# Attention over packed queries with a feed-forward block: another order of the first batch's steps, two more fillers' worth of matmuls at the start, some pieces on another engine

## The chip, the cores and the metric

The kernel runs on one core of one Trainium2 chip. The metric is the device time of one execution in microseconds. The core has the engines TensorE (PE; its weight loads are shown apart, as PEld), VectorE (DVE), ScalarE (ACT) and GpSimd (POOL), and SyncE (SP), which issues the transfers. Each works through its own list of instructions in order and waits on semaphores for the others.

## The reference

For 8 batches of 8 heads, 576 tokens and a head size of 64, 32 packed queries per head attend to all tokens, and then the tokens attend to the 32 packed results:

```python
def sm_attn(qq, kk, vv):
    s = scale * np.matmul(qq, kk.transpose(0, 1, 3, 2))
    s = s - np.max(s, axis=-1, keepdims=True)
    a = np.exp(s)
    a = a / (np.sum(a, axis=-1, keepdims=True) + 1e-09)
    return np.matmul(a, vv)
p_packed = sm_attn(p, k, v)
out = sm_attn(q, p_packed, p_packed)
```

The output (4608 tokens by 512) goes through a block of 2048 hidden features, whose weights are given in 64 bits:

```python
h = x @ w_in
g = h * (1.0 / (1.0 + np.exp(-1.702 * h)))
return (g @ w_out).astype(np.float32)
```

## The kernel before, in words

All steps are small functions, and one tuple, `order` (line 709 on), lists them with their arguments: 2856 steps. A loop calls them one after the other. Each engine takes its instructions in that order, so the table alone decides what stands behind what on PE, DVE, ACT, POOL and in SP's list of transfers. The first argument of most steps is the batch; steps of the feed-forward part then have the block f of 128 hidden features (16 of them) and the token half (288 tokens).

One batch goes like this. `load` fetches keys with packed queries (`k`), values (`v`, in a long piece of four chunks and a short one, `v_last`) and queries (`q`). `scores1_first`, `max1_first`, `bias1` and `exp1_first` do the first softmax of batch 0 straight from PSUM; for later batches `scores1_mm`, `scores1_copy`, `scores1_max` and `exp1` do. `turn1_mm`, `turn1_copy` and `turn1_last_*` transpose the weights of batch 0 into `aT`; for later batches `turn1_blocks`, `turn1_out` and `turn1_in` take them through device memory. `pack` multiplies with v, `pack_end` and `pack_turn_*` scale and transpose the result (`PT`). `scores2_mm`, `scores2_turn`, `max2`, `sub2`, `exp2`, `sum2`, `norm2` and `turn2` do the second softmax in a token-major layout, in halves, the first token half in its even and odd heads apart. The second product with the packed result is not carried out: `m_chunk` multiplies PT with a chunk of w_in (512 features; the first chunk of batch 0 in two column halves), and `h_mm` multiplies the second softmax's weights with that.

Every matmul operand of the large products is split into a high part (a cast) and a low part (the difference), and a product is three matmuls. `m_upper` and `m_lower` split m, `a_upper`, `a_lower`, `a_lower_mm` and `a_lower_copy` the weights, `h_upper` and `h_lower` the activated block, `upper_w` and `lower_w` a block of w_out. `h_tanh` (ACT) and `h_gate`, `h_over` (DVE) make the activation; the bank of h comes free behind them. There are two such banks (`psh`), two further ones for passing use (`psb`), and four that accumulate the output. `out_mm` adds one block's product to one of the four.

The weights come in raw 64-bit form: `load_w` fetches a piece, `begin_w` (ACT) and `join_w` (DVE) turn it into 32 bits. Pieces 0 to 3 are w_in's first chunk, 4 to 7 the first blocks of w_out, 8 to 11 w_in's second chunk. A piece of the first chunk comes in two column halves. SP issues all transfers; from the ninth on a transfer also waits until the one eight places ahead of it has landed.

`warm` (line 121) issues n matmuls of 128 by 128 that nobody reads, as fillers. An engine given as the last argument (`dve`, `act`, `pool`) says who does a cast, copy or difference; without it, ACT casts and POOL subtracts.

## Time and profile before

| | us |
|---|---|
| median of 3 runs | 697.97 (697.94 to 698.82) |
| span of the profiled execution | 695.4 |
| PE busy in it | 685.3 |
| DVE busy in it | 439.1 |
| ACT busy in it | 258.1 |
| POOL busy in it | 96.1 |

The span goes from the first to the last instruction of the profiled execution; its own time around that span is not listed apart, so the median stands 2.57 us above the span. A busy time is the sum over an engine's instructions; pieces of one engine overlap a little at their ends, so that a sum of durations is somewhat more than the distance from start to start. Times in the rows below are from the start of the span.

### The profile page before, as it was taken

What the parts mean: (1) busy time and instruction counts of PE and PEld (TensorE: products, weight loads), DVE (VectorE), ACT (ScalarE), POOL (GpSimd) and SP (SyncE); (2) the same over time, 40 slices, a digit from 0 to 9 for tenths busy, and PEclk for the clock granted to TensorE, in tenths of its full rate; (3) what the DMA queues carried; (4) which work ended last, traced back from release to release, by engine and by line L of the source; (5) the groups of instructions that cost most, each with busy time, mean ns of one, the idle gap of its engine ahead of it and who ended that gap; (6) DMA issues with size and microseconds to landing.
All of it is one profiled execution on the core that took longest, in us unless ns stands there. A gap on an engine that the chain in (4) does not pass through costs nothing.

```text
span 695.4 us, 12968 instructions
## 1 busy us (share of the span) xinstructions
PE 685.3 (99%) x5022; PEld 561.1 (81%) x5022; DVE 439.1 (63%) x1111; ACT 258.1 (37%) x620; POOL 96.1 (14%) x115
## 2 busy tenths in 40 slices
PE   7999999999999999999999999999999999999997
PEld 5688788888888888887888878888888887878885
DVE  4988784536555467555686477766785647855443
ACT  3876554423314324433323233332232333333220
POOL 2554372112300224011000000000000000000000
PEclk9999999999999999999999999999999999999999
DMA  8989703432101511064000623034200160010001
GB/s 336 375 307 240 283 1 107 93 113 77 65 1 30 184 65 54 16 155 160 1 31 6 156 56 131 16 110 111 96 16 1 37 177 1 23 40 1 1 15 61
DMA packets 55260, 65.18 MB, mean 94 GB/s; under 512 B 35808, under 2 KB 40864, under 8 KB 54176
## 3 DMA queue, kind: packets, MB, share of 16 engines
q1 hardware_dynamic: 55120, 64.23, 29.2%
q8 instruction: 40, 0.66, 0.4%
q14 instruction: 20, 0.16, 0.1%
q10 hardware_dynamic: 80, 0.13, 0.0%
HBM read 50.78 MB, written 13.57 MB: 93 GB/s over the span
## 4 chain that ended last, share of the span: by engine, by line
PE 93%; DMA 3%; DVE 1%; issue 1%; SPq 1%; ACT 0%; DVEq 0%; ACTq 0%
PE acc L665 50%; PE h L605 28%; PE acc_over L665 5%; PE psm_None L437 4%; DMA aT<-aside 2%; PE pspv L408 1%; PE ps L250 1%; PE ps L495 1%; DMA k<-pk 1%; PE warm L125 1%; SPq L384 1%; DMA aside<-xb 0%; DVE ghi L119 0%; DVE x L506 0%; PE pst L345 0%
## 5 line engine op out<-in xcount | busy, mean ns | idle before, releaser
L665 PE MATMUL acc<-wo,ghi 128*128 128x512 f32 x1024 | 322.9, 397 | 0.0
L665 PEld LDWEIGHTS acc<-wo,ghi 128*128 128x128 f32 x1024 | 179.8, 188 | 40.2 <-issue 11.2
L613 ACT ACTIVATE g<-h 128x288 f32<-128x288 f32 x256 | 104.1, 410 | 278.1 <-PE h L605 262.1
L665 PE MATMUL acc<-wo,glo 128*128 128x512 f32 x512 | 202.0, 395 | 0.0
L595 DVE SCALAR_TENSOR_TENSOR g<-g,h 128x288 f32<-128x288 f32 (+1 forms) x256 | 104.9, 415 | 116.4 <-ACT g L613 115.8
L605 PE MATMUL h<-ahi,mhi 128*128 128x288 f32 x496 | 140.1, 298 | 0.3 <-DVE g L595 0.3
L605 PE MATMUL h<-ahi,mlo 128*128 128x288 f32 x496 | 138.9, 296 | 0.0
L665 PEld LDWEIGHTS acc<-wo,glo 128*128 128x128 f32 x512 | 96.2, 188 | 22.8 <-POOL glo L592 0.4
L605 PEld LDWEIGHTS h<-ahi,mhi 128*128 128x128 f32 x496 | 93.4, 188 | 16.2 <-DVE x L506 4.9
L605 PE MATMUL h<-alo,mhi 128*128 128x288 f32 x496 | 105.2, 293 | 0.0
L605 PEld LDWEIGHTS h<-ahi,mlo 128*128 128x128 f32 x496 | 93.5, 189 | 6.9
L592 DVE TENSOR_TENSOR glo<-g,ghi 128x224 fp32r<-128x224 f32 (+1 forms) x183 | 76.1, 427 | 14.8 <-ACT ghi L117 10.8
L592 POOL TENSOR_TENSOR glo<-g,ghi 128x224 fp32r<-128x224 f32 (+1 forms) x73 | 55.5, 767 | 191.3 <-DVE ghi L119 88.1
L605 PEld LDWEIGHTS h<-alo,mhi 128*128 128x128 f32 x496 | 79.7, 188 | 0.1
L117 ACT CAST ghi<-g 128x288 fp32r<-128x288 f32 (+1 forms) x142 | 55.2, 403 | 54.4 <-DVE g L595 47.6
L595 DVE SCALAR_TENSOR_TENSOR over<-g,h 128x64 f32<-128x64 f32 x128 | 27.0, 214 | 30.6 <-ACT g L613 30.1
L471 DVE TENSOR_TENSOR mlo<-psm_None,mhi 128x512 fp32r<-128x512 f32 x60 | 40.6, 684 | 5.2 <-ACT mhi L117 4.9
L119 DVE CAST ghi<-g 128x224 fp32r<-128x224 f32 (+1 forms) x114 | 35.9, 320 | 7.0 <-PE acc L665 1.4
L665 PE MATMUL acc_over<-wo,ghi_over 128*128 128x512 f32 x128 | 39.9, 393 | 0.0
L117 ACT CAST mhi<-psm_None 128x512 fp32r<-128x512 f32 x45 | 26.2, 584 | 29.3 <-PE psm_None L437 29.3
L437 PE MATMUL psm_None<-w_in,PT 64*32 64x512 f32 x496 | 33.4, 597 | 0.0
L665 PEld LDWEIGHTS acc_over<-wo,ghi_over 128*128 128x128 f32 x128 | 23.6, 188 | 4.8
(95 smaller groups left out, 475.9 us busy)
## 6 DMA issues: line engine op xcount, KB each, us to landing
q<-q SPq DMA_DIRECT2D x16, 576.0 KB, 5.8
v<-v SPq DMA_DIRECT2D x8, 1024.0 KB, 6.2
o<-o SPq DMA_DIRECT2D x32, 256.0 KB, 2.6
raw<-w_out SPq DMA_DIRECT2D x16, 511.8 KB, 6.5
raw<-w_in SPq DMA_DIRECT2D x12, 511.8 KB, 8.9
k<-pk SPq DMA_DIRECT2D x8, 640.0 KB, 4.3
k<-pk SPq DMA_DIRECT2D x8, 576.0 KB, 6.9
aside<-xb SPq DMA_DIRECT2D x56, 72.0 KB, 2.3
```

Source lines behind the costliest of these rows:

```text
L117: nc.scalar.copy(dst, src)
L119: engine.tensor_copy(dst, src)
L125: nc.tensor.matmul(t[:, :P], ident, ident, start=True, stop=True)
L250: nc.tensor.matmul(bank[32 * j : 32 * j + 32, :NH], kq["p", b][rows(eo), j, :], kq["k", b][rows(eo), half, j, :], start=True, stop=True,)
L384: nc.sync.dma_start(d[:, :, NP * eo + j, :], src.rearrange("t (g n) -> t g n", n=NPK))
L437: nc.tensor.matmul(banks[eo][32 * j : 32 * j + 32, columns(part)], PT[rows(eo), j, :], w_in_sb[fc][rows(eo), j, columns(part)], start=True ...
L471: nc.vector.tensor_tensor(lo, bank[:, at], hi.bitcast(F32), op=ALU.subtract)
L592: engine.tensor_tensor(lo, src, hi.bitcast(F32), op=ALU.subtract)
L595: nc.vector.scalar_tensor_tensor(dst, th, 1.0, h, op0=ALU.add, op1=ALU.mult)
L605: nc.tensor.matmul(h[:, :NH], m[eo][part][:, fo : fo + P], a[:, eo * NH : (eo + 1) * NH], start=(n == 0), stop=(n == len(terms) - 1),)
L613: nc.scalar.activation(g, st["h", b, f, half][:, :NH], AF.Tanh, scale=1.702)
L665: nc.tensor.matmul(acc, gp[:, at : at + P], wo[f][:, part, :], start=(start and i == 0), stop=(stop and i == 2),)
```

## The change

The table is written anew from its first step up to step 399 of the list (in the old one) and is the same from there on, where the second scores of batch 1 begin. No function changes. Of the table a few lines:

```diff
     order = (
-        (load, "k", 0, 0), (warm, 7, 3), (load, "k", 0, 1), (scores1_first, 0), (max1_first, 0, 0),
-        (scores1_first, 1), (max1_first, 0, 1), (bias1, 0, 0), (load_w, 0, 0), (max1_first, 1, 0),
...
+        (load, "k", 0, 0), (load, "k", 0, 1), (warm, 7, 7), (scores1_first, 0), (warm, 1, 1),
+        (scores1_first, 1), (max1_first, 0, 0), (max1_first, 0, 1), (bias1, 0, 0), (warm, 2, 3),
...
```

The first filler has 7 matmuls instead of 3, and a filler of one is new between the two halves of the first scores. The other fillers keep their lengths and change places; two of three matmuls each stand ahead of the first transposes now, and none between m's first chunk and the first scores of batch 1.

Forty-odd pieces are given to another engine. In the start-up: `turn1_copy` (both) and `pack_turn_copy` of batch 0 and the second `a_lower_copy` go from DVE to ACT; the subtraction `sub2` of the second token half goes from DVE to POOL; `a_upper` of the second token half goes from ACT to DVE, its `a_lower` and `lower_w` of piece 4 go from POOL to DVE. In the rest of the batch, casts of pieces 6, 20, 21, 23, of three activated half blocks and one of m go from DVE to ACT, the low parts of pieces 14, 15, 21, 22 and of one half block from DVE to POOL; other casts (three of m, of pieces 13 and 14, and of six half blocks, and `pack_turn_copy` of batch 1) go to DVE from ACT, and the low parts of piece 20 and of eight half blocks to DVE from POOL.

On SP, the first transfers of w_in change places, and the short piece of v goes ahead of the long one. (Names: `raw` a piece of weights, `k`, `q`, `v` the inputs.) Before:

```order
L189 DMA raw_131<-w_in 128x1023
L151 DMA v_157<-v 128x2048
L153 DMA v_157<-v_last 128x512
L189 DMA raw_231<-w_in 128x1023
L157 DMA q_235<-q 128x1152 x2
L189 DMA raw_254<-w_in 128x1023
L189 DMA raw_277<-w_in 128x1023
L189 DMA raw_131<-w_in 128x1023
L189 DMA raw_254<-w_in 128x1023
```

Now:

```order
L189 DMA raw_141<-w_in 128x1023
L153 DMA v_155<-v_last 128x512
L151 DMA v_155<-v 128x2048
L189 DMA raw_177<-w_in 128x1023
L157 DMA q_189<-q 128x1152
L189 DMA raw_252<-w_in 128x1023
L157 DMA q_189<-q 128x1152
L189 DMA raw_262<-w_in 128x1023
L189 DMA raw_252<-w_in 128x1023
L189 DMA raw_177<-w_in 128x1023
```

The first piece is now piece 2 (before piece 0), the first half of piece 3 stands between the halves of q, and the second half of piece 3 ahead of the second half of piece 0.

On DVE, in the second softmax of batch 0 (`sm`, `rs`: sums and their reciprocals; `x`: the weights; `xt`: the same turned; `w_in`: a joined piece). Before:

```order
L539 TENSOR_REDUCE sm_0_0_304<-x_0_0_238 128x9
L540 TENSOR_SCALAR sm_0_0_304<-sm_0_0_304 128x9
L541 RECIPROCAL rs_0_0_305<-sm_0_0_304 128x9
L530 TENSOR_TENSOR x_0_1_262<-x_0_1_262,mx_0_1_275 128x576
L539 TENSOR_REDUCE sm_0_0_304<-x_0_0_238 128x9
L540 TENSOR_SCALAR sm_0_0_304<-sm_0_0_304 128x9
L541 RECIPROCAL rs_0_0_305<-sm_0_0_304 128x9
L539 TENSOR_REDUCE sm_0_1_323<-x_0_1_262 128x18
L540 TENSOR_SCALAR sm_0_1_323<-sm_0_1_323 128x18
L541 RECIPROCAL rs_0_1_324<-sm_0_1_323 128x18
L220 SCALAR_TENSOR_TENSOR w_in_79<-raw_254,tops 128x256
L551 STREAM_TRANSPOSE xt_0_351<-x_0_0_238 128x288 x2
```

Now:

```order
L539 TENSOR_REDUCE sm_0_0_298<-x_0_0_241 128x9
L540 TENSOR_SCALAR sm_0_0_298<-sm_0_0_298 128x9
L541 RECIPROCAL rs_0_0_299<-sm_0_0_298 128x9
L220 SCALAR_TENSOR_TENSOR w_in_79<-raw_177,tops 128x256
L539 TENSOR_REDUCE sm_0_0_298<-x_0_0_241 128x9
L540 TENSOR_SCALAR sm_0_0_298<-sm_0_0_298 128x9
L541 RECIPROCAL rs_0_0_299<-sm_0_0_298 128x9
L539 TENSOR_REDUCE sm_0_1_347<-x_0_1_266 128x18
L540 TENSOR_SCALAR sm_0_1_347<-sm_0_1_347 128x18
L541 RECIPROCAL rs_0_1_348<-sm_0_1_347 128x18
L551 STREAM_TRANSPOSE xt_0_365<-x_0_0_241 128x288 x2
```

The subtraction of the second half (L530) is gone to POOL, a join has come in between, and the join ahead of the transposes is behind them.

On DVE around the first gates (`g`: the activated block, named by half and f; `dec`: a joined piece of w_out; `alo`, `ahi`: parts of the softmax's weights). Before:

```order
L220 SCALAR_TENSOR_TENSOR w_in_79<-raw_231,tops 128x256
L220 SCALAR_TENSOR_TENSOR w_in_79<-raw_277,tops 128x256
L595 SCALAR_TENSOR_TENSOR g_0_0_401<-g_0_0_401,h_0_0_394 128x288
L294 TENSOR_REDUCE mx_1_0_338<-x_1_0_337 128x1
L595 SCALAR_TENSOR_TENSOR g_0_1_430<-g_0_1_430,h_0_1_423 128x288
```

Now:

```order
L119 CAST ahi_1_428<-xt_1_412 128x576
L220 SCALAR_TENSOR_TENSOR w_in_79<-raw_262,tops 128x256
L595 SCALAR_TENSOR_TENSOR g_0_0_426<-g_0_0_426,h_0_0_394 128x288
L574 TENSOR_TENSOR alo_1_429<-xt_1_412,ahi_1_428 128x576
L220 SCALAR_TENSOR_TENSOR dec<-raw_367,tops 128x512
L220 SCALAR_TENSOR_TENSOR dec<-raw_344,tops 128x512
L595 SCALAR_TENSOR_TENSOR g_0_1_448<-g_0_1_448,h_0_1_416 128x288
```

A low part and two full-width joins stand between the first two gates now. On PE the four h products of the first two blocks now all come ahead of the first `out_mm`, where one `out_mm` stood between them before; piece 4, which the first `out_mm` needs, is loaded after pieces 5 and the last keys of batch 1. Further on, `h_over` of block 3 stands behind three joins and another block's gate on DVE, and PE's `h_mm` of block 2, second half, needs the bank that it frees.

## Rows read from the trace of the kernel before

**Rows 1.** The page, one engine's busy time, share and instructions:
```profile
PE 685.3 (99%) x5022; PEld 561.1 (81%) x5022; DVE 439.1 (63%) x1111; ACT 258.1 (37%) x620; POOL 96.1 (14%) x115
```
**Rows 2.** Windows: length, busy PE, PEld, DVE, ACT, POOL (instructions), clock, DMA share, GB/s:
```profile
14.00:25.00 11.00, 9.83 (x110) 6.43 (x109) 10.21 (x29) 6.51 (x17) 4.13 (x5) 1.00 1.03 405
25.00:36.00 11.00, 11.00 (x88) 8.73 (x87) 10.31 (x25) 10.33 (x24) 6.88 (x6) 1.00 0.79 310
```
**Rows 3.** Order of time, PE: start, us, line, operation, times, idle before:
```profile
1.37 1.65 PE L125 MATMUL warm<-ident 128*128 128x128 f32 x6 [1.37 <-POOL ident masks.py:199]
...
6.13 1.22 PE L250 MATMUL ps<-k 64*32 64x288 f32 x16 [0.20 <-DMA k<-pk]
...
16.16 1.60 PE L125 MATMUL warm<-ident 128*128 128x128 f32 x12
```
**Rows 4.** SP's issues, and four answers on issues: KB, us to landing:
```profile
1.65 0.43 SPq L189 DMA_DIRECT2D raw<-w_in  x1
raw<-w_in SPq DMA_DIRECT2D x1, 255.8 KB, 6.8
2.80 0.45 SPq L153 DMA_DIRECT2D v<-v_last  x1
v<-v_last SPq DMA_DIRECT2D x1, 256.0 KB, 8.8
9.28 0.47 SPq L189 DMA_DIRECT2D raw<-w_in  x1
raw<-w_in SPq DMA_DIRECT2D x1, 255.8 KB, 7.8
```
**Rows 5.** ACT's first exponent, PE's pack, and ACT's copies of one bank, mean ns:
```profile
8.23 0.50 ACT L314 ACTIVATE x<-ps,nb 128x288 f32<-128x288 f32 x1 [5.80 <-DVE nb L303]
...
11.50 1.57 PE L408 MATMUL pspv<-v,aT 128*32 128x64 f32 x80
...
L117 ACT COPY o<-acc 128x512 f32<-128x512 f32 x2 | 1.2, 580 | 0.0
```
**Rows 6.** Order of time, DVE, second softmax of batch 0:
```profile
15.03 0.85 DVE L506 STREAM_TRANSPOSE x<-ps 128x288 f32<-128x288 f32 x2 [0.53 <-PE ps L495]
...
19.51 0.70 DVE L530 TENSOR_TENSOR x<-x,mx 128x576 f32<-128x576 f32 x1
...
22.14 0.36 DVE L220 SCALAR_TENSOR_TENSOR w_in<-raw,tops 128x256 uint32<-128x256 uint32 x1
22.42 0.82 DVE L551 STREAM_TRANSPOSE xt<-x 128x288 f32<-128x288 f32 x2
...
24.92 0.46 DVE L119 CAST alo<-psal 128x288 fp32r<-128x288 f32 x1
```
**Rows 7.** Order of time, ACT, ahead of the first h:
```profile
22.73 0.80 ACT L208 CAST tops<-raw 128x512 f16<-128x512 bf16 x1
23.37 0.78 ACT L117 CAST ahi<-xt 128x288 fp32r<-128x288 f32 x2
```
**Rows 8.** Order of time, PE behind the first h, and a wait:
```profile
25.77 0.71 PE L250 MATMUL ps<-k 64*32 64x288 f32 x16
...
44.69 0.19 PEld L605 LDWEIGHTS h<-ahi,mhi 128*128 128x128 f32 x1 [0.52 <-DVE g L595]
```
**Rows 9.** Order of time, DVE pieces beside POOL's subtraction:
```profile
25.99 1.29 DVE L220 SCALAR_TENSOR_TENSOR w_in<-raw,tops 128x256 uint32<-128x256 uint32 x2
...
40.72 0.31 DVE L119 CAST ghi<-g 128x288 fp32r<-128x288 f32 x1
...
41.95 1.76 POOL L232 TENSOR_TENSOR wo<-dec,wo 128x512 fp32r<-128x512 f32 x1
42.48 1.37 DVE L119 CAST ghi<-g 128x224 fp32r<-128x224 f32 x1
```
**Rows 10.** The chain that ended last: start, us, what:
```profile
64.23 5.90 DMA aT<-aside
...
70.15 1.32 PE pspv L408 x80
```

More of the change, by code (lines that the diff above doesn't have):

```diff
@@ new lines @@
+        (load, "q", 0, 0), (join_w, 0, 0), (pack, 0, 0, late), (pack, 0, 1), (pack_end, 0),
+        (pack_turn_mm, 0), (pack_turn_copy, 0), (scores2_mm, 0, 0), (load_w, 3, 0), (warm, 9, 3),
+        (begin_w, 3, 0), (load, "q", 0, 1), (join_w, 3, 0), (scores2_turn, 0, 0, 0),
+        (load_w, 1, 0), (load_w, 3, 1), (load_w, 0, 1), (scores2_mm, 0, 1, late), (begin_w, 3, 1),
+        (scores2_turn, 0, 0, 1), (begin_w, 1, 0), (max2, 0, 0, 0), (warm, 6, 2),
+        (sub2, 0, 0, 0, pool), (max2, 0, 0, 1), (scores2_turn, 0, 1, 0), (sub2, 0, 0, 1, pool),
@@ new lines @@
+        (load, "v", 2, 1), (h_upper, 1, 2, 0), (h_lower, 1, 2, 0), (m_upper, 1, 1, 1, None),
+        (m_lower, 1, 1, 1), (out_mm, 1, 0, 0), (out_mm, 1, 0, 2), (out_mm, 1, 1, 2),
+        (h_mm, 1, 2, 1), (h_upper, 1, 3, 0), (h_lower, 1, 3, 0, dve), (h_upper, 1, 3, 1),
+        (h_mm, 1, 4, 1), (h_tanh, 1, 2, 1), (out_mm, 1, 1, 1), (h_over, 1, 2), (h_gate, 1, 2, 1),
+        (out_mm, 1, 1, 0), (h_mm, 1, 5, 0), (h_upper, 1, 2, 1), (h_tanh, 1, 4, 1),
+        (h_gate, 1, 4, 1), (h_over, 1, 4), (h_lower, 1, 3, 1, dve), (store, 0, 0),
@@ L968 @@
[L968 removed]
+        (out_mm, 2, 0, 2), (m_chunk, 2, 1), (m_upper, 2, 1, 1, None, dve),
+        (h_lower, 2, 2, 1, dve), (m_upper, 2, 1, 0, None), (m_lower, 2, 1, 0),
+        (scores1_mm, 3, 0, inner), (scores1_copy, 3, 0, 0), (out_mm, 2, 0, 0), (load, "k", 3, 1),
+        (store, 1, 2), (scores1_copy, 3, 0, 1, dve), (h_mm, 2, 3, 1), (h_tanh, 2, 3, 1),
+        (h_gate, 2, 3, 1), (out_mm, 2, 1, 2), (h_lower, 2, 2, 0, dve), (h_mm, 2, 3, 0),
@@ new lines @@
+        (turn1_in, 3, 4), (turn1_in, 3, 5), (pack, 3), (h_mm, 2, 10, 0), (sum1, 3, 0),
+        (pack_end, 3), (pack_turn_mm, 3), (pack_turn_copy, 3, dve), (h_mm, 2, 9, 0),
+        (h_tanh, 2, 10, 0), (h_tanh, 2, 9, 0), (h_gate, 2, 9, 0), (h_gate, 2, 10, 0),
+        (out_mm, 2, 8, 1), (m_chunk, 2, 3), (m_upper, 2, 3, 0, None), (h_upper, 2, 9, 0),
+        (m_lower, 2, 3, 0), (h_upper, 2, 9, 1), (h_lower, 2, 9, 1), (load, "q", 3, 0),
+        (load, "q", 3, 1), (scores2_mm, 3, 0, inner), (scores2_turn, 3, 0, 0), (out_mm, 2, 7, 2),
@@ new lines @@
+        (scores2_mm, 4, 0, inner), (scores2_turn, 4, 0, 0), (h_upper, 3, 8, 1),
+        (h_lower, 3, 8, 1), (store, 2, 3), (scores2_turn, 4, 0, 1), (max2, 4, 0), (m_chunk, 3, 3),
+        (m_upper, 3, 3, 0, None), (h_mm, 3, 10, 0), (h_tanh, 3, 10, 0),
+        (m_upper, 3, 3, 1, None, dve), (m_lower, 3, 3, 1), (out_mm, 3, 7, 0), (m_lower, 3, 3, 0),
+        (h_gate, 3, 10, 0), (h_upper, 3, 9, 1), (h_lower, 3, 9, 1, dve), (out_mm, 3, 8, 0),
+        (sub2, 4, 0, None, pool), (load, "q", 4, 1), (out_mm, 3, 7, 2), (out_mm, 3, 8, 2),
```

890 lines of the change are left out of this document (437 added, 453 removed).

## The prediction

> **What bounds the kernel now.** I read the page first: PE is busy 685.3 of 695.4 us [rows 1], so only what keeps PE from useful matmuls can move the time. The order of the steps differs only up to the end of the first batch's tenth block of hidden features; behind that both kernels run the same list. The busy time by stretch says where PE has slack: in 14 to 25 us PE is busy 9.83 of 11.00, much of that with fillers, while DVE has 10.21 of 11.00; in 25 to 36 us PE, DVE and ACT are all full (11.00, 10.31, 10.33) [rows 2]. So the time is: the moment at which PE gets its first steady work, plus what it waits after that, plus matmul work that the change leaves alone. The order of time then gives the start-up chain: scores of the first batch, exponents, transposes, pack, second scores, softmax on DVE and POOL, and the first block of h. That block ends when PE takes up the scores of batch 1 at 25.77 us [rows 8]. This is the mark against which I measure the change.
>
> **The start, 0 to 15 us.** PE's first three fillers take 1.65 us from 1.37 us, 0.275 us a pass (two passes a matmul); at 16.16 us twelve passes take 1.60 us, 0.133 us each [rows 3]. The clock column of the windows reads 1.00 in every stretch, but the same instruction at half the pace is the 1.2 GHz level; by the same rows PE works at that level at least up to the fillers of 7.27 us, after work from 1.37 to 3.0 and from 4.71 us on. Seven fillers at 0.55 us end at 5.2 us, where the first scores began at 4.71 before. If the pace stays low, they, the added filler (0.55) and the second scores (1.22 us [rows 3]) end near 8.0 us instead of 7.35; if it doubles by 6 us, near 7.1. That is +0.7 to -0.25 us at the first maximum. I price it at nothing, because two other things are later anyway. First, ACT now decodes the first piece of w_in before the exponents. The transfer in that place lands at 1.65 + 6.8 = 8.45 us [rows 4], so the exponents start at about 8.45 + 0.4 = 8.85 us instead of 8.23 [rows 5]. Second, the short piece of v now goes ahead of the long one. The short one was down at 2.80 + 8.8 = 11.6 us [rows 4], the long one earlier; now the long one comes last, at 11.6, and pack's first matmul needs it, where pack could start at 11.50 before [rows 5]. The two copies of transposed weights go from DVE to ACT (0.58 us each by ACT's copy of the same size [rows 5]). Behind the exponents, at 10.9 us, the two and the copy of the last piece are done at about 12.4 us. Pack's last piece of the even heads waits for that, and pack ends at about 13.35 instead of 13.07 us (+0.3). A copy moved to ACT and a join of w_in that now stands ahead of DVE's first transpose keep that shift: the transposes start at about 15.3 us instead of 15.03 [rows 6]. **+0.27 us**, between +0.1 and +0.7.
>
> **DVE's softmax, 15 to 22 us.** DVE works without a break here, so the sum goes by starts. A join of a half-width piece leaves the place ahead of the transposes: -0.28 us (22.14 to 22.42; it is busy 0.36, so pieces overlap by 0.08). The subtraction of the second half at 19.51 us moves to POOL: -0.62 us (0.70 less the same 0.08) [rows 6]. Two more joins only change places (one earlier, one later, 0.33 each, zero). The transposes of the first half then start at 0.62 + 0.28 - 0.27 = 0.63 us earlier, at 21.8 instead of 22.42. The cover for the moved piece: POOL has to subtract and ACT to take the exponent while DVE goes through the two sums of the first half; if that is too little, the gain shrinks by what is missing. ACT now waits for another transfer before the first exponent, since a decode of the second half of piece 3 stands ahead of it. The transfer in that place lands at 9.28 + 7.8 = 17.08 us [rows 4], so the exponent starts near 17.8 us and ends at 18.25, 0.3 us before DVE needs it. If these 0.3 us are gone, every further delay counts in full. **-0.90 us** for the stage, between -0.9 and -0.3.
>
> **The first h, 22 to 26 us.** Before, the low part of the second half came last, by a DVE cast at 24.92 us (0.46 us) [rows 6] behind four other pieces. Now ACT takes both low parts, and DVE has only the two m_lower behind its transposes. ACT's chain becomes the bound. It begins with the copy of batch 1's first scores at about 20.4 us (they follow m's first chunk now without the six fillers between), and ten pieces stand in it: one full-width decode (0.64 us to the next start, 22.73 to 23.37), nine casts, copies and half-width decodes of about 0.35 us (two take 0.78) [rows 7]; 20.4 + 0.64 + 9 x 0.35 = 24.2 us. With the last h products behind that the first h ends near 24.45 us against 25.77 [rows 8]: **-1.3 us** in total at this mark, between -1.9 (ACT's decodes cover nothing) and -0.5 (a transfer of batch 1's keys or of w_out comes half a microsecond late and ACT waits for it).
>
> **Full load, 24 to 46 us.** Here I expect a part to be given back, since the work that DVE must do before PE can go on has grown. The high and the low part of the second token half and the low part of the first w_out block come to DVE: 0.70 us each by DVE's 128x576 subtraction [rows 6], 2.1 us, against 0.46 us that left. Two places matter. The second h of the second token half needs the bank that gate (0, 1, 0) frees; that gate stands behind two full-width joins (about 0.65 us each, twice the half-width one) and comes at about 27.7 us, done at 28.1, while PE has finished the rest at about 27.4: +0.7 us. Before, PE had an out product to do here; now the first of these waits for a w_out block that is loaded four places later in SP's list. Then h (0, 2, 1) needs the bank of h (0, 3, 1). The last reader of that is over (0, 3), now behind the gate of another block and three joins on DVE, of which the last waits for ACT's decode: about 35.4 us, where PE arrives at about 34.6: +0.8 us. On the other side the kernel before has waits of its own at the end of this stretch: the weight load at 44.69 us stood 0.52 us for a DVE gate [rows 8], and with the slow issue around it I count 0.7 us by the pitch of an h product (0.78 us). In the new order the gates stand nearer to their h there. The stretch: +0.7 + 0.8 - 0.7 = **+0.8 us**, between -0.7 (no wait) and +2.5.
>
> On DVE and POOL there is a row to weigh. A DVE cast that took 0.31 us at 40.72 took 1.37 us at 42.48, until just behind the end of POOL's subtraction at 41.95 + 1.76 = 43.71 us; two joins at 25.99 us took 1.29 us together [rows 9], where one takes 0.36 at 22.14 [rows 6], so 0.57 us more than twice that. The Trainium skill, page "SBUF — State Buffer", section "SBUF: two separate sides", says that DVE and GpSimd share one port pair, held for a whole instruction by whoever starts first, while the other fully blocks. The trace agrees, by the 1.37 us. By that rule a piece that goes from POOL to DVE costs DVE less than its busy time, and DVE's joins beside POOL cost more. For the two waits above it would give +0.5 us more (one join held behind the first glo piece), a time of 698.0.
>
> **Behind that, to 120 us.** In the rest of the first batch some twenty casts and low parts change sides; DVE gains about 2.4 us of work over 65 us in which PE never waited long. I take zero, between -0.2 and +1.5. The transfers that turn batch 1's weights through memory are reordered too. Before, the last of them landed at 64.23 + 5.90 = 70.13 us and pack began at 70.15 [rows 10], just in time. In the new order the long piece of v goes ahead of them and only three weight blocks between, so that the last should land near 66 us: hidden, and worth up to 0.2 us. If it came later than 70 us, PE would wait for it in full.
>
> **Rivals.** *The lead is kept* (no wait at the two gates): 697.97 - 1.3 - 0.7 = 695.97, say 695.9 us. For it: DVE's total in 24 to 36 us is hardly larger and it starts 0.6 us earlier. Against it: the gate is behind two joins by order, which no speed of PE changes. *The gain is used up* (POOL's subtraction or the transfer at 17.08 us late, then one wait): 697.97 - 0.5 + 0.5 = 698.0 us; this is also the case where the filler and the order do nothing. *Slower: DVE is the bound in 26 to 37 us.* Eight joins stand there beside POOL's low parts; if four meet one and each loses the 0.57 us of the joins at 25.99 [rows 9], that is 2.3 us more before the banks of (0, 1, 0) and (0, 3, 1) come free: 697.5 + 2.3 = 699.8 us. It decides as soon as DVE loses more than the 0.5 us that are left of the lead. For it: DVE's 10.31 of 11.00 us there [rows 2]. Against it: POOL gives up 2.1 us' worth of DVE's new pieces, so it is idle more often beside the joins. The Trainium skill's page "SBUF — State Buffer", section "SBUF: two separate sides", has the rule by which it would happen.
>
> **How the numbers follow.** The sum against the profiled span: 695.4 - 1.3 + 0.8 = 694.9 us. The three runs have a median of 697.97, 2.57 us above the span, for what lies around it; with that the forecast is 697.5 us. A difference under 0.2%, 1.4 us, is about what a measurement of this kernel can't tell from no change: faster is below 696.57, slower above 699.37. Forecast 697.5 (own range 696.6 to 698.9): 0.50. Lead kept, 695.9: 0.21. Used up, 698.0: 0.11. DVE the bound, 699.8: 0.18. Faster 0.21 + 0.03 from the forecast's lower tail = 0.24; slower 0.18 + 0.01 = 0.19; same 0.57. The range goes from 695.8 to 699.9, the ends of the two outer cases; it leaves out about 1 in 10 at each side, for the unknown waits.
>
> **What would show it.** Right: exponents at about 8.85 us, pack after 11.6 us, the first-half transposes to the token layout near 21.8 us, the scores of batch 1's second half at about 24.5 us, PE waits for DVE at about 27.5 and 35 us. Wrong: a first h not earlier than 25.2 us (then ACT or a transfer is the bound), no wait for DVE in 27 to 36 us (the lead is kept), or PE waits of over 0.5 us behind 46 us, above all for the transfers into aT.

## The result, and the profile after

| | before | after |
|---|---|---|
| median | 698.23 us (697.2 to 698.99, 20 runs) | 700.4 us (698.63 to 702.27, 20 runs) |
| span of the profiled execution | 695.4 us | 697.5 us |

The ratio is 1.0034, with a 95% interval of [1.0027, 1.0041]: slower by 2.2 us, more than the 0.2% that tell a difference from none. The forecast was 697.5 us, in a range of 695.8 to 699.9.

Not all of the 2.2 us lies in the span. The record has time and span of every execution of the changed kernel, and of over a hundred of before that ran beside the experiments. For before the time is 1.79 us above the span in the median (1.73 to 1.95), for the changed kernel 2.46 (2.40 to 2.49). So **0.66 us are lost outside the span**, where no trace looks, and 1.55 in it: the median span went from 696.4 to 697.95. The profiled execution of before, with 695.4, was a quick one.

The changed kernel's page (each engine's busy time, share and instructions), then the two stretches of [rows 2]:

```profile
PE 687.9 (99%) x5032; PEld 561.4 (80%) x5032; DVE 439.7 (63%) x1117; ACT 257.8 (37%) x619; POOL 91.7 (13%) x110
```
```profile
14.00:25.00 11.00, 9.51 (x108) 6.48 (x108) 9.70 (x26) 6.20 (x17) 4.98 (x6) 1.00 1.03 391
25.00:36.00 11.00, 10.81 (x89) 8.75 (x88) 10.35 (x25) 10.75 (x26) 5.04 (x5) 1.00 0.94 368
```

DVE has half a microsecond less to do up to 25 us (9.70, 10.21 before), as meant, but PE gets nothing of it. Order of time on PE, the lines that answer to [rows 5], [rows 8] and [rows 10] (start, us, line, operation, idle before):

```profile
11.39 1.57 PE L408 MATMUL pspv<-v,aT 128*32 128x64 f32 x80
...
25.85 0.71 PE L250 MATMUL ps<-k 64*32 64x288 f32 x16
...
29.14 0.40 PE L605 MATMUL h<-ahi,mhi 128*128 128x288 f32 x1 [0.19 <-DVE g L595]
...
69.42 1.32 PE L408 MATMUL pspv<-v,aT 128*32 128x64 f32 x80
...
86.03 1.03 PE L495 MATMUL ps<-q,PT 64*32 64x288 f32 x16 [0.55 <-DVE g L595]
```

The scores of batch 1's second half start at 25.85 us, where 24.45 was forecast and before had 25.77. Of the two waits forecast in 24 to 46 us, one is there with 0.19 us, the other not at all. The last line is half of the second scores of batch 1, which stood at 85.20 us before:

```profile
85.20 0.69 PE L495 MATMUL ps<-q,PT 64*32 64x288 f32 x16
```

From there on the order of the steps is that of before, and PE still loses more. To see it I set the starts of PE's instructions against those of the first trace of before, one by one, and took the median difference in windows of 15 us. The difference is 1.11 us at 92 to 99 us and 2.39 us at 655: **1.28 us are lost in work that the change doesn't touch.** Such a difference is worked out from the whole order of time; the table below gives it for all traces. The last three columns have its growth, that is, how much later PE gets than it was at 92 to 99 us.

| trace | second-half scores of batch 1 | second scores, first half | at 92 to 99 us against the first trace of before | growth to 302 us | to 452 us | to 655 us |
|---|---|---|---|---|---|---|
| before | 25.77 | 74.46 | 0 | 0 | 0 | 0 |
| b_again | 25.99 | 75.79 | +1.26 | +0.01 | -0.01 | -0.05 |
| b_pt_dve | 26.24 | 76.49 | +1.97 | -0.03 | -0.11 | -0.22 |
| b_warm7 | 25.88 | 76.08 | +1.55 | -0.01 | -0.02 | -0.16 |
| b_warm1 | 26.57 | 75.69 | +1.15 | -0.10 | -0.16 | -0.34 |
| b_phase | 25.76 | 75.59 | +1.06 | -0.03 | +0.33 | +0.35 |
| b_layout | 26.09 | 75.65 | +1.11 | +0.48 | +0.63 | +0.78 |
| after | 25.85 | 74.57 | +1.11 | +0.50 | +0.95 | +1.28 |
| a_join26 | 26.00 | 75.38 | +0.86 | +0.56 | +0.97 | +1.18 |
| a_pt_act | 26.65 | 78.71 | +4.18 | +0.51 | +0.57 | +0.66 |
| a_warm_old | 25.96 | 75.72 | +1.17 | +0.43 | +0.82 | +1.01 |
| a_exp26 | 26.60 | 76.28 | +1.75 | +0.56 | +0.92 | +1.24 |
| a_b31 | 26.58 | 75.26 | +0.74 | +0.37 | +0.80 | +1.09 |
| a_sub_dve | 27.14 | 77.57 | +3.04 | +0.44 | +0.58 | +0.75 |
| a_phase | 25.54 | 75.77 | +1.25 | +0.48 | +0.62 | +0.81 |
| a_layout | 26.52 | 75.89 | +1.36 | -0.06 | +0.26 | +0.39 |
| a_both | 25.63 | 76.09 | +1.54 | -0.04 | -0.05 | -0.03 |
| a_both31 | 25.96 | 76.36 | +1.83 | -0.06 | -0.10 | -0.08 |

(Names with b_ are the kernel before with one edit, with a_ the changed kernel with one.) Two things stand in it. Up to 99 us one execution differs from the next by a microsecond: the kernel before itself, run again, is 1.26 us later there, and before's seven traces go from 0 to 1.97. The first trace of before was a quick one, and the +1.11 of the changed kernel's is no effect of the change. Leaving out the four kernels whose start or transfers went another way (a_pt_act, a_exp26, a_b31, a_sub_dve) and a_both31, the six changed kernels have a mean of 1.22 us and the seven of before 1.16. **The whole rearrangement is worth nothing at 92 us**, as far as this scatter lets one see. Behind 99 us, instead, the four further traces with before's lists (b_pt_dve's differ by one entry) and places stay within 0.35 us of it, and after, a_join26 and a_warm_old grow by 1.0 to 1.3 us. A little comes back at the very end: from the end of PE's last product to the end of the span it is 4.50 us in all eleven traces of the changed table and 4.82 in all seven of before's. The experiments are told in the order in which theories fell.

### The profile page after: what moved, and what is told of

It is laid out like the page before. It is cut to its first block, busy times and chain, and to the rows that moved or that the text cites. A ratio compares the mean times of both kernels' runs of the same rounds, so it can differ in the third digit from the quotient of the medians.

```text
span 697.5 us, 12984 instructions
## 1 busy us (share of the span) xinstructions
PE 687.9 (99%) x5032; PEld 561.4 (80%) x5032; DVE 439.7 (63%) x1117; ACT 257.8 (37%) x619; POOL 91.7 (13%) x110
## 4 chain that ended last, share of the span: by engine, by line
PE 93%; DMA 2%; DVE 2%; issue 1%; ACT 1%; SPq 0%; POOL 0%; POOLq 0%; DVEq 0%; ACTq 0%
PE acc L665 50%; PE h L605 28%; PE acc_over L665 5%; PE psm_None L437 4%; PE ps L250 1%; PE pspv L408 1%; DMA raw<-w_in 1%; PE ps L495 1%; DMA raw<-w_out 1%; PE warm L125 1%; DVE dec L220 1%; ACT tops L208 0%; DVE g L595 0%; DVE w_in L220 0%; DVE wo L119 0%
## 5 line engine op out<-in xcount | busy, mean ns | idle before, releaser
L592 DVE TENSOR_TENSOR glo<-g,ghi 128x288 fp32r<-128x288 f32 (+1 forms) x190 | 79.9, 432 | 15.4 <-ACT ghi L117 11.0
L117 ACT CAST ghi<-g 128x224 fp32r<-128x224 f32 (+1 forms) x139 | 54.1, 402 | 55.8 <-DVE g L595 49.1
L592 POOL TENSOR_TENSOR glo<-g,ghi 128x288 fp32r<-128x288 f32 (+1 forms) x66 | 50.4, 769 | 184.7 <-DVE ghi L119 86.0
L119 DVE CAST ghi<-g 128x288 fp32r<-128x288 f32 (+1 forms) x117 | 36.6, 318 | 7.0 <-PE acc L665 1.4
L208 ACT CAST tops<-raw 128x512 f16<-128x512 bf16 (+1 forms) x36 | 24.5, 713 | 12.6 <-DMA raw<-w_in 9.0
```

The source lines that it names most:

```text
L117: nc.scalar.copy(dst, src)
L119: engine.tensor_copy(dst, src)
L208: nc.scalar.copy(top[n, part].bitcast(F16).rearrange("p (n h) -> p n h", h=2)[:, at, 1], raw[slot_of(queue[n])].bitcast(BF16).rearrange("p ...
L592: engine.tensor_tensor(lo, src, hi.bitcast(F32), op=ALU.subtract)
```

## Experiments: a late block of w_out

The first theory was a wait at 82 to 86 us. The chain of the profiled execution after (start, us, what):

```profile
74.17 0.68 DVE w_in L220
...
75.64 6.49 DMA raw<-w_out
82.15 0.79 ACT tops L208
...
86.03 1.03 PE ps L495 x16
```

And what stood ahead of the first of these on DVE:

```profile
73.97 0.29 DVE L119 COPY PT<-pspt 128x128 f32<-128x128 f32 x1 [1.11 <-PE pspt L427]
```

DVE waits 1.11 us for a copy that the change gave to it; the join of piece 26 stands behind it, frees a buffer late, and the load that needs the buffer lands at 82.1 us, where before it was at 79.5. The edits move the join ahead of the copy, or the copy back to ACT, or put the copy alone on DVE in the kernel before; a fourth run is before once more.

```diff
-(pack_turn_mm, 1), (pack_turn_copy, 1, dve), ... (scores2_mm, 1, 0, inner), (join_w, 26),
+(pack_turn_mm, 1), (join_w, 26), (pack_turn_copy, 1, dve), ... (scores2_mm, 1, 0, inner),   [a_join26]
-(pack_turn_copy, 1, dve)
+(pack_turn_copy, 1)                                                                         [a_pt_act]
-(pack_turn_copy, 1)
+(pack_turn_copy, 1, dve)                                                                    [b_pt_dve]
```

> The changed kernel with one step moved: the join of weight piece 26 stands ahead of the copy of batch 1's packed result on DVE instead of behind it. Theory A (late load): in the changed kernel DVE waits 1.11 us for PE's transpose ahead of that copy, so the join starts at 74.17 us instead of 73.62 before, the two loads of w_out behind it are issued at 74.89 and 75.64 us instead of 74.33 and 74.70, the second lands at 82.1 us instead of 79.5, ACT waits 1.54 us for it with an activation behind it, and PE reaches the second half of batch 1's second scores at 86.03 us where before it was 85.20. With the join ahead it starts at about 72.9 us, the second load lands by 80 us, ACT does not wait, and the time falls by 0.9 to 1.2 us, to about 699.3 us. Theory B (pace): the loss is spread over the whole run (the distance between the two traces grows by 1.2 us from 87 to 630 us without a step), and the step at 86 us is one profile's accident: the time stays at 700.4 us.

> The changed kernel with one engine put back: the copy of batch 1's packed result is ACT's again. Theory A (late load): DVE's join of piece 26 is free from 72.9 us on, as in the run with the join ahead of the copy; about 699.3 us, and the same as that run within 0.3 us. Theory B (pace): 700.4 us. If this one gains and the run with the join moved doesn't, it is ACT against DVE for the copy itself (0.29 us on DVE) and not the wait that stands in front of the join.

> The kernel before with the one engine changed: the copy of batch 1's packed result goes to DVE, ahead of the join of piece 26. Theory A (late load): DVE waits for PE's transpose at about 73 us, the join of piece 26 slips from 73.62 to about 74 us or later, the loads with it, and the time rises by up to 1.1 us, from 698.2 to between 698.6 and 699.3 us. Theory B (pace): no change, 698.2 us.

> The kernel before once more, unchanged, for a second trace of it. Both theories: 698.2 us. It tells how far two traces of one kernel drift apart from the same mark on: if the second trace of before is up to 1 us later at 630 us than at 87 us against the first, without a step, then the 1.2 us of drift between before and after is the scatter of single executions; if they agree within 0.3 us, the slower pace belongs to the changed kernel.

Measured: a_join26 699.59 us, 1.0025 [1.0017, 1.0034]; a_pt_act 699.32, 1.0023 [1.0010, 1.0036]; b_pt_dve 698.35, 1.0000 [0.9992, 1.0009]; b_again 698.33, 0.9998 [0.9990, 1.0007]. The wait of PE is gone in a_join26 (86.07, no idle time), and still 1.2 to 1.4 us of the slowdown are left. A later run, a_warm_old, has the old place of the join and the same wait on DVE, and its loads came in time all the same:

```profile
75.12 0.29 DVE L119 COPY PT<-pspt 128x128 f32<-128x128 f32 x1 [1.12 <-PE pspt L427]
...
81.63 1.42 ACT L208 CAST tops<-raw 128x512 f16<-128x512 bf16 x2
```

So the copy is not the cause; some executions meet a late block there, others not. What its share is in the median of after is open: the joins' and the copy's versions lie 0.8 to 1.1 us below it, but so does a_warm_old (699.69), and the intervals overlap.

One execution shows how dear such a wait can be. In a_pt_act's trace a block lands late and PE waits for ACT's high part; PE, then three stretches with the columns of [rows 2], the granted clock behind POOL's:

```profile
73.67 0.73 PE L665 MATMUL acc<-wo,ghi 128*128 128x512 f32 x2 [1.18 <-ACT ghi L117]
```
```profile
70.00:74.00 4.00, 2.82 (x87) 2.03 (x86) 3.72 (x10) 2.20 (x8) 1.27 (x1) 1.00 0.47 185
74.00:77.00 3.00, 2.88 (x9) 1.96 (x8) 2.23 (x6) 0.69 (x2) 0.60 (x1) 0.64 0.00 0
77.00:80.00 3.00, 3.00 (x38) 1.53 (x36) 0.47 (x2) 0.78 (x2) 1.34 (x2) 0.79 0.92 304
```

PE stood idle for 1.18 us ahead of 73.67, and behind it the mean clock is 0.64 and 0.79 for 6 us: these are means of stretches that lie in part at the level of 1.2 GHz and in part at 2.4. Single out products took 0.63 us there (at 75.68 and 76.96), and 0.40 at 72.09 and 78.38. The trace is 3 us behind the others at 92 to 99 us (+4.18), more than twice the wait.

The mean granted clock of every execution is on record, and tells how often this happens. It is 0.997 in this trace's execution; 0.997 or less stands in 24 of the 123 executions of kernels with the changed table, in none of the 67 of kernels with b_, and in one of over a hundred of before. Of the changed kernel's own 20 executions it is 6, of the 24 of a_join26 and a_warm_old none. This is a part of what parts their medians, and not all: the other 14 of after have a median of 700.24 us.

## Experiments: the fillers

The changed kernel's first filler and the one between the first scores, taken back, and each put alone into before:

```diff
-(warm, 7, 7)   (warm, 1, 1)
+(warm, 7, 3)                  [a_warm_old]
-(warm, 7, 3)
+(warm, 7, 7)                  [b_warm7]
+(warm, 1, 1)                  [b_warm1]
```

> The changed kernel with the fillers' lengths of before: the first has three matmuls again and the one between the first scores is gone. From 92 us on, the traces of three kernels with the changed order fall behind before by the same 0.6 to 1.4 us, a few hundredths at a time and at the same instructions, where two more traces of before's order keep their distance within 0.1 us. Theory P (PE's list): ten more matmul passes, or the one more bank taken from the pair of h, shift where the later list stands; without them the drift is gone (under 0.2 us from 92 to 670 us) and the time falls by about 1.2 us, to 699.2 us. Theory O (the order of the first batch leaves the other engines or the buffers in another phase): the drift stays at 0.6 to 1.4 us and the time at 700.4 us.

> The kernel before with the first filler of seven matmuls instead of three, nothing else: eight more passes on PE, the same number of banks. Theory P by the position of the instructions: a drift of 0.6 to 1.4 us from 92 to 670 us and about 699.4 us. Theory P by the pair of banks, or theory O: no drift, 698.3 us; the longer filler alone costs nothing if PE still waits for the keys after it, and up to 0.5 us if the first scores start later.

> The kernel before with the filler of one matmul between the two halves of the first scores, nothing else: two more passes on PE, and one bank more taken in turn from the pair that h uses, so that every later block of h stands in the other bank. Theory P by the pair of banks: a drift of 0.6 to 1.4 us from 92 to 670 us and about 699.4 us. Theory P by position: little drift (two passes instead of ten). Theory O: no drift, 698.3 us. The filler itself puts the second half of the first scores back by up to 0.5 us, of which the first exponent sees nothing if the first maximum waits for DVE anyway.

Measured: a_warm_old 699.69 us, 1.0022 [1.0012, 1.0032]; b_warm7 697.79, 0.9995 [0.9985, 1.0005]; b_warm1 698.70, 1.0002 [0.9993, 1.0012]. The fillers are worth nothing that can be measured, alone or together, and the growth stays without them (+1.01 in a_warm_old) and doesn't come with them (-0.16 and -0.34 in the other two).

## Experiments: the place in an engine's list

At 391 us the changed kernel's trace falls back by a single step of 0.2 us, and at 439 and 628 by 0.1 each; b_phase, below, falls back at the same places. In b_again and then in b_phase, an h product's end on PE, the activation behind it on ACT, and the weight load that waits for ACT:

```profile
387.29 0.42 PE L605 MATMUL h<-alo,mhi 128*128 128x288 f32 x2
...
388.09 0.88 ACT L613 ACTIVATE g<-h 128x288 f32<-128x288 f32 x2 [1.36 <-PE h L605]
...
391.24 0.30 PEld L665 LDWEIGHTS acc<-wo,ghi 128*128 128x128 f32 x2 [0.19 <-ACT ghi L117]
```
```profile
387.06 0.42 PE L605 MATMUL h<-alo,mhi 128*128 128x288 f32 x2
...
387.56 0.41 ACT L613 ACTIVATE g<-h 128x288 f32<-128x288 f32 x1 [1.07 <-PE h L605]
...
389.35 0.42 PE L605 MATMUL h<-alo,mhi 128*128 128x288 f32 x2
...
390.13 0.41 ACT L613 ACTIVATE g<-h 128x288 f32<-128x288 f32 x1 [1.39 <-PE h L605]
...
391.19 0.30 PEld L665 LDWEIGHTS acc<-wo,ghi 128*128 128x128 f32 x2 [0.46 <-ACT ghi L117]
```

The first activation starts 0.38 us behind the end of its h in b_again (387.71 to 388.09) and 0.08 in b_phase; the next one 0.36 us behind in b_phase. The late one is in both the 576th entry of ACT's list, if the semaphore waits are counted as entries. Starts that are 0.11 to 0.35 us later than that of the same piece at another number stand also at ACT's entries 192, 704 and 832 and at DVE's 1088 and 1216: all odd multiples of 64. Not every one has it (ACT's 448 hasn't), and none shows at the even ones 640 and 768. From the 250th entry on I compared each piece's start behind its release in b_phase and b_again. They differ by over 0.15 us only at ACT's 576 and 832, at one piece right behind 832, and at DVE's 1216. The change makes ACT's list 4 entries shorter and DVE's 4 longer, so from then on the late start falls on other pieces, and on some that PE waits for (the weight load of the last line waits 0.46 us, that of b_again 0.19). b_phase gives four early casts of before from ACT to DVE, which moves both lists as the change does; a_phase gives four of the changed kernel back:

```diff
-(upper_w, 13), (upper_w, 14), (upper_w, 15), (h_upper, 0, 5, 0)
+(upper_w, 13, dve), (upper_w, 14, dve), (upper_w, 15, dve), (h_upper, 0, 5, 0, dve)   [b_phase]
-(pack_turn_copy, 1, dve), (upper_w, 22, dve), (h_upper, 0, 10, 0, dve), (h_upper, 0, 8, 0, dve)
+(pack_turn_copy, 1), (upper_w, 22), (h_upper, 0, 10, 0), (h_upper, 0, 8, 0)           [a_phase, beside a_join26's]
```

> The kernel before with four casts of the first batch given from ACT to DVE (w_out's pieces 13, 14 and 15 and the activated block 5, first half): ACT's list is 4 shorter and DVE's 4 longer at the common part, as in the changed kernel, the order is that of before. Theory L (place in the list): a drift of 1.0 to 1.3 us from 92 to 670 us against before, at the same instructions as in the changed kernel (0.25 us at ACT's 192nd and 832nd), and about 699.4 us. Theory O: no drift, 698.3 us. The four casts themselves, about 0.43 us each on DVE between 45 and 60 us, may cost up to 0.4 us ahead of 92 us, which the marks there tell apart.

> The changed kernel with the join of piece 26 ahead of the copy (699.59 us) and four casts of the first batch's end given back from DVE to ACT (the copy of batch 1's packed result, the cast of w_out's piece 22, and those of two activated half blocks), so that ACT's and DVE's lists are as long at the common part as in the kernel before: 4 more on ACT and 4 fewer on DVE. Theory L (place in the list): in the changed kernels ACT's activation comes 0.25 to 0.28 us late at its 192nd and 832nd instruction (waits on semaphores counted), DVE's at its 1216th, and in before ACT's at its 576th; all are multiples of 64, and the four instructions' shift moves the gap to another piece of work. With the lists shifted back the drift from 92 to 670 us, 1.0 to 1.3 us in the changed kernels, is under 0.2 us, and the time falls to about 698.5 us. Theory O (another state left by the first batch: buffers, the transfers' list): the drift stays over 0.8 us and the time at 699.6 us.

Measured: b_phase 698.77 us, 1.0010 [1.0001, 1.0018]; a_phase 699.40, 1.0017 [1.0008, 1.0025]. In the traces the growth behind 302 us is +0.38 in b_phase and +0.33 in a_phase, against -0.06 in b_again and +0.62 in a_join26: the place in the lists is worth 0.3 to 0.4 us, made in the one and taken away in the other. Of the medians b_phase's agrees: its median span is 696.8 us, 0.4 over before's. a_phase's can't be told from a_join26's, and the 0.2 us by which it is lower lie outside the span (2.22 us there instead of 2.46; the spans are 697.20 and 697.15). That time outside the span follows the edits of the lists as well, 2.20 to 2.23 us in the three changed kernels with lists as long as before's (a_phase and, below, a_both and a_both31) and 2.00 in b_phase; what is done there isn't shown. Two other kernels change the lists' lengths by the way, a_pt_act and a_sub_dve, and they lose that step as well (+0.06 and +0.14 from 302 to 452 us, where after has +0.45).

## Experiments: the place of the tiles in memory

The 0.5 us up to 302 us stay in a_phase. There no instruction is later than another by a step; the products are longer, the out products above all. Groups by line, 120 to 690 us (busy us, mean ns, idle), of b_again, b_layout and the changed kernel, in that order:

```profile
L665 PE MATMUL acc<-wo,ghi 128*128 128x512 f32 x882 | 277.8, 396 | 0.0
```
```profile
L665 PE MATMUL acc<-wo,ghi 128*128 128x512 f32 x882 | 278.2, 397 | 0.0
```
```profile
L665 PE MATMUL acc<-wo,ghi 128*128 128x512 f32 x882 | 278.3, 397 | 0.0
```

These rows alone would not settle it, since the first trace of before has 278.0. But the instructions are the same, and the places of their tiles are not: the pool lays its groups of buffers out in the order of their first use, and the changed table uses them in another order. (No view lists addresses; that they differ follows from this order.) The edit takes the groups once ahead of the table, in the order of the other kernel, and changes no instruction:

```diff
+for tag, shape, dt, n in (("kqv", ..., 2), ("x", ..., 6), ...):
+    for _ in range(n):
+        wk.tile(shape, dt, tag=tag, name=f"hold_{tag}", bufs=n)
 order = (
```

b_layout is before with the changed kernel's places, a_layout a_join26 with those of before, a_both a_phase with those of before.

> The kernel before with its tiles laid out in SBUF as in the changed kernel: each group of buffers is reserved ahead of the list, in the order in which the changed kernel first uses them; no instruction is added or moved. Theory M (place in memory): a drift of 0.6 to 0.8 us from 92 to 670 us against before, most of it between 110 and 300 us, and 698.9 to 699.0 us. Theory O (another state of the first batch, such as which buffer of a group is whose, or POOL's and SP's lists): no drift, 698.2 us.

> The changed kernel with the join of piece 26 ahead of the copy (699.59 us), and its tiles laid out as in before. Theory M: of the drift of 1.2 us from 92 to 670 us about 0.4 us is left, the part that follows the place in ACT's and DVE's lists (from 380 us on); 698.8 us. Theory O: the drift stays at 1.0 to 1.3 us, 699.6 us.

> The changed kernel with the join of piece 26 ahead of the copy, the four casts given back to ACT (lists as long as in before, 699.4 us) and the tiles laid out as in before. Theory M with the lists' place: the drift from 92 to 670 us is under 0.2 us, and the time 698.4 us, what before takes. Theory O: the drift stays at 0.7 to 0.8 us and the time at 699.4 us.

Measured: b_layout 699.12 us, 1.0017 [1.0008, 1.0026]; a_layout 699.45, 1.0018 [1.0006, 1.0030]; a_both 698.83, 1.0016 [1.0003, 1.0029]. The traces are plain: before with the other places grows by 0.78 us, the changed kernel with the places of before by 0.39 instead of 1.18, and with both edits by -0.03. The two parts add up: 0.78 + 0.35 = 1.13 of 1.18.

They can also be told apart in one trace, by the size of the steps. I compared the distance from each start on PE to the next one, from 99 to 655 us, with that in b_again. In differences of less than 0.06 us each, the nine kernels with the changed places gain 0.67 to 0.92 us in sum, the others -0.28 to +0.06 (a_layout 0.05, a_both 0.02). In larger steps, all at 389 to 392, 439 and 628 us, the seven kernels with lists that are four entries apart gain 0.36 to 0.39 us (a_layout 0.39, b_phase 0.37), and b_layout, a_phase and a_both have no such step.

The median of b_layout shows its part (+0.9 us, the interval is clear of 1, and all of it in the span). a_layout's doesn't: it lies 0.1 us below a_join26's, where 0.8 was to be won. a_both's lies 0.8 us below, with overlapping intervals; its median span of 696.6 us is 0.2 over before's, and the rest of what it still lacks (0.4 us) lies outside the span. Which buffers matter, and why a place costs, isn't shown: of b_layout's 0.81 us in small differences 0.43 stand in the products with the high part ghi, 0.24 in the other out products and 0.13 in those of h with alo, 0.3 to 0.5 ns a product.

## Experiments: the start

What became of DVE's gain, and could more be had? Three kernels beside a_join26: the decodes of pieces 1, 3 and 0 behind the exponents (a_exp26), only that of the second half of piece 3 behind the exponent (a_b31), and the subtraction back on DVE (a_sub_dve); a_both31 is a_both with a_b31's edit.

```diff
-(begin_w, 3, 1), (scores2_turn, 0, 0, 1), (begin_w, 1, 0), ... (exp2, 0, 0, 0), ... (begin_w, 0, 1), (join_w, 1, 0), ... (exp2, 0, 0, 1), (sum2, 0, 0, 0),
+(scores2_turn, 0, 0, 1), ... (exp2, 0, 0, 1), (begin_w, 1, 0), (begin_w, 3, 1), (begin_w, 0, 1), (sum2, 0, 0, 0), (join_w, 1, 0),   [a_exp26]
-(begin_w, 3, 1), (scores2_turn, 0, 0, 1), ... (exp2, 0, 1),
+(scores2_turn, 0, 0, 1), ... (exp2, 0, 1), (begin_w, 3, 1),   [a_b31]
-(sub2, 0, 1, None, pool)
+(sub2, 0, 1, None)   [a_sub_dve]
```

> The changed kernel with the join of piece 26 ahead of the copy (as in the first run, 699.59 us) and one more change in the start: ACT takes the two exponents of the first token half ahead of the decodes of the second half of piece 3 and of piece 1, and DVE's join of piece 1 goes behind the first sum. In the changed kernel ACT waits 3.35 us, up to 17.75 us, for the transfer of piece 3's second half, the first exponent starts at 18.44 us (17.07 before) and DVE waits 0.57 us ahead of its join. Theory A (the transfer took the gain): the exponent starts at about 17.0 us, DVE's sums at 18.05 us, the transposes near 21.6 us instead of 22.58, the first block of h ends near 25.0 us instead of 25.85, and if PE keeps that lead the time falls by 0.8 us to about 698.8 us. Theory B (ACT's own chain of copies and casts, or the fillers, bound the first h): the transposes come earlier, but PE takes up the scores of batch 1 at 25.6 us or later and the time stays at 699.6 us. Theory C (the lead is used up at the gates between 27 and 36 us): the first h at 25.0 us, but PE takes up the second scores of batch 1 no earlier than 75.2 us; 699.6 us.

> The changed kernel with the join of piece 26 ahead of the copy and one decode moved on ACT: the second half of piece 3 behind the exponent of the second token half, the rest as it was. Theory A (the transfer of that half took the gain): ACT decodes piece 1 at about 17.0 us, the first exponent starts by 17.5 us instead of 18.44, DVE's join doesn't wait, and the distance from DVE's first transposes to the turn of the weights falls from 7.70 us to about 7.0 us. Theory S (POOL's subtraction of the second half holds DVE): DVE waits less, but one piece beside the subtraction (18.1 to 19.3 us) takes 0.6 us longer than elsewhere, and the distance stays at 7.4 us or more, as in before (7.39). Time: 699.6 us if PE's scores of batch 1 stay at 25.8 to 26.0 us, up to 0.6 us less if they come earlier.

> The changed kernel with the join of piece 26 ahead of the copy and one piece back on DVE: the subtraction of the second token half (POOL: 1.16 us; DVE: 0.70 us). Theory S (POOL's subtraction holds DVE for about as long as DVE saves): the distance from DVE's first transposes to the turn of the weights stays within 0.2 us of the changed kernel's 7.70 us, though DVE has 0.62 us more to do; the join of piece 1 takes 0.4 us instead of 0.95. Theory N (nothing is lost beside POOL): the distance grows by 0.6 us to 8.3 us and the time by up to 0.6 us over 699.6 us.

> As the kernel with both, and the decode of the second half of piece 3 moved on ACT behind the exponent of the second token half. Theory M: no drift; the distance from DVE's first transposes to the turn of the weights is 6.9 us as in the run with that decode moved, and the time is that of the kernel with both, 698.4 us, or up to 0.5 us less if PE keeps what DVE gains. Theory O: a drift of 0.7 to 0.8 us, 699.4 us.

Measured: a_exp26 700.72 us, 1.0037 [1.0021, 1.0052]; a_b31 699.86, 1.0036 [1.0022, 1.0050]; a_sub_dve 701.30, 1.0041 [1.0028, 1.0054]; a_both31 697.93, 1.0002 [0.9993, 1.0012]. In a_exp26 the join of piece 1 came late and PE waited 1.09 us for it at 20.41 us. In a_sub_dve the stage from the first transposes to the token layout is 0.7 us longer (7.61 us, 6.90 to 7.00 in a_join26 and a_phase), the subtraction's own time, so POOL is the better place for it. a_sub_dve's time tells less: in its trace the mean granted clock is 0.51 from 11.5 to 15.0 us, behind a wait of PE of 1.32 us at 9.81, and three of its five executions have a mean of 0.997. But against before the move gives less than 0.7 us. Order of time in a_phase, two pieces of DVE of one form and POOL's subtraction:

```profile
19.22 0.65 DVE L540 TENSOR_SCALAR sm<-sm 128x9 f32<-128x9 f32 x1
...
20.83 0.17 DVE L540 TENSOR_SCALAR sm<-sm 128x9 f32<-128x9 f32 x1
```
```profile
18.57 1.27 POOL L530 TENSOR_TENSOR x<-x,mx 128x576 f32<-128x576 f32 x1 [0.52 <-DVE mx L526]
```

A piece of 0.17 us took 0.65, to 19.87, just behind POOL's end at 19.84: 0.48 us of DVE's time went with the subtraction that left it. The Trainium skill, page "SBUF — State Buffer", section "SBUF: two separate sides", has the rule for it (the port pair that DVE and GpSimd share is held for a whole instruction by whichever starts first); the trace agrees, by the 0.48 us. With the subtraction on DVE the stall is not gone, it falls on a join beside POOL's next piece: in a_sub_dve 0.90 us at 21.47, beside a norm of 1.00 at 21.08, where such a join took 0.36 [rows 6].

a_both31 is the best version with the new table: 697.93 us, below after (their intervals don't meet) and not to be told from before. It isn't shown that its early decode does anything, since a_b31 alone is no better than a_join26; the drift it lacks is that of a_both.

## Why the prediction was wrong, point by point

**The start, +0.27: right in size.** ACT's first exponent and DVE's first transposes after:

```profile
8.47 0.49 ACT L314 ACTIVATE x<-ps,nb 128x288 f32<-128x288 f32 x1
```
```profile
14.88 0.85 DVE L506 STREAM_TRANSPOSE x<-ps 128x288 f32<-128x288 f32 x2
```

The exponents are later by 0.24 us in this trace [rows 5], where 0.6 was forecast (8.85 us). But each of the eleven changed kernels starts them 0.43 to 0.59 us behind the landing of the first piece of w_in, which scatters from 7.47 to 9.07 us, and their mean is 8.88 against 8.34 in the seven of before: +0.54, as forecast, and by the wait that was forecast. The transposes are earlier in this trace (14.88, forecast 15.3), because its pack began at 11.39; pack scatters from 10.7 to 12.4 us with the transfers, with a mean of 11.87 us in eleven changed kernels against 11.48 in seven of before: +0.39.

**DVE's softmax, -0.90: mis-sized, about -0.4.** From the first transposes to the first half's token layout it is 7.39 us in before's trace (22.42 - 15.03), and 7.70 in the changed kernel's:

```profile
17.75 0.82 ACT L208 CAST tops<-raw 128x256 f16<-128x256 bf16 x2 [3.35 <-DMA raw<-w_in]
18.44 0.43 ACT L534 ACTIVATE x<-x 128x288 f32<-128x288 f32 x1
```
```profile
18.60 0.95 DVE L220 SCALAR_TENSOR_TENSOR w_in<-raw,tops 128x256 uint32<-128x256 uint32 x1 [0.57 <-ACT tops L208]
...
22.58 0.78 DVE L551 STREAM_TRANSPOSE xt<-x 128x288 f32<-128x288 f32 x2
```

The transfer came at 17.75, not at 17.08, and the 0.3 us of cover that the prediction named were gone: the exponent ends at 18.87 and the join at 18.60 had waited 0.57 us and took 0.95 beside POOL's subtraction. In four of seven traces of this table's start the join doesn't wait, DVE's L540 is held for 0.48 us instead, as in a_phase, and the distance is 6.9 to 7.0 us; in three the join waits, and it is 7.7. The mean is 7.26 against 7.64 in the seven of before. The step left out that the moved piece holds DVE's port where it now stands (0.48 of its 0.62 us); I weighed that rule for the joins at 26 us and not for the subtraction itself.

**The first h, -1.3 in total: wrong, about 0.** From the token layout to the scores of batch 1 it took 3.35 us before, and 3.27 now (22.58 to 25.85). The -0.67 rested on a sum of ACT's ten pieces. But ACT is not full:

```profile
23.04 0.79 ACT L117 CAST ahi<-xt 128x288 fp32r<-128x288 f32 x2 [0.23 <-DVE xt L551]
...
24.45 0.40 ACT L117 CAST alo<-psal 128x288 fp32r<-128x288 f32 x1 [0.33 <-PE psal L567]
25.06 0.40 ACT L117 CAST alo<-psal 128x288 fp32r<-128x288 f32 x1 [0.22 <-PE psal L567]
```

It waits for the transposes, then twice for PE's psal products. The chain from transposes over casts and psal to the copies sets the end, and to shorten ACT's or DVE's list does nothing to it. "Wrong: a first h not earlier than 25.2 us" was the right test, but the cause isn't the bound that it named.

**Full load, 24 to 46 us, +0.8: wrong, 0.** From the scores of batch 1 to its second scores the six changed kernels take 49.65 us in the mean, the seven of before 49.64. The gate of (0, 1, 0) costs PE 0.19 us at 29.14, not 0.7, and nothing is waited for at 35 us, not 0.8; nor is before's own wait of 0.52 [rows 8] won as 0.7: after has one of 0.29 us at 51.30 us. These two errors, -1.3 and +0.8, nearly cancelled, so the forecast for 46 us was only 0.5 us off.

**To 120 us, zero: right in the mean.** The transfers into aT are hidden, with pack at 69.42 (70.15 before [rows 10]).

**"Behind that both kernels run the same list": the step that failed.** It was true of the steps and taken to mean no time. The same list costs 1.0 to 1.3 us more, by its place in the engines' lists (0.3 to 0.4) and by that of its tiles in memory (0.78). The second term taken over unchanged was the 2.57 us above the span "for what lies around it". For before it was in truth 1.79, beside a quick trace, which does no harm to the sum; but in the changed kernel it is 0.66 us more, less the 0.32 by which the span ends sooner behind PE's last product. Why both change isn't shown. Without the lead of 0.5 that never came, 697.97 + 1.2 + 0.66 - 0.32 gives 699.5, with a_join26's 699.6 and a_warm_old's 699.7 beside it. Of the 2.2 us of after, the 0.7 to 0.8 above those two aren't explained; a wait for a late block, as in its trace, and the executions with a lower granted clock are the candidates. Of the rivals, "the gain is used up", by POOL's subtraction or the transfer at 17.08 us, is what happened up to 92 us; "DVE is the bound" gave the nearest time, 699.8, by a mechanism that the trace doesn't show.

## What to carry to other kernels

A kernel that fills PE to 99% gets nothing from an earlier piece unless the chain behind it is followed to its end: each release, and not the sum of an engine's list, sets the next start. When a reordered beginning makes the untouched rest slower, compare the rest instruction by instruction, and try the same places in memory and the same lengths of the lists before searching for a wait. One trace per kernel isn't enough where a difference is under 0.3%: here two executions of one kernel lay 1.3 us apart at 92 us. And a time that is measured around the span can change outside it: compare time and span of each execution before a trace is asked to explain the whole difference.

## What the runs showed of the hardware

- Entries 192, 576, 704 and 832 of ACT's list and 1088 and 1216 of DVE's, waits counted, started 0.11 to 0.35 us late, whichever piece stood there. It costs where PE waits for that piece (the weight load waited 0.46 us instead of 0.19 at 391 us).
- The same matmuls with their tiles laid out in another order took 0.78 us longer over 560 us, in differences of less than 0.06 us each; with the old order it was gone (0.02 us in a_both).
- A wait of 1.18 us on PE was followed by 6 us at a mean granted clock of 0.64 and 0.79 (a_pt_act), one of 1.32 us by a mean of 0.51 from 11.5 to 15.0 us (a_sub_dve).
- The time outside the span is not the same for all kernels: 1.79 us for before, 2.46 for the changed kernel.
- A block of w_out of 512 KB landed 4.8 us after its issue in before's trace (issued at 74.70) and 6.5 us after it in after's (75.64). What held the second one isn't shown.
